# Backward pass of a cached attention block on one core: the last twenty value-cache heads taken two by two

## The chip, the cores and the metric

The kernel runs on one core of a Trainium2 chip. The metric is device time in microseconds for one execution of the whole program, given as the median of several runs. A profiled execution gives, beside its time, a trace of every instruction and DMA packet. The engines of the core are named as in the profile: PE (TensorE, matrix products), PEld (its weight loads), DVE (VectorE), ACT (ScalarE), POOL (GpSimd), SP (SyncE, which only issues loads here). Sixteen DMA engines move data between HBM and the on-chip memory.

## The reference

A pre-norm block with attention over a cache and a small dense layer, for a batch of 2 and one new position, 32 heads of 128, a cache of 4096 positions. The kernel computes the output and all gradients for a given output gradient.

```
def _fwd_reference(A_x, A_k_cache, A_v_cache, A_wq, A_wo, B_x, B_w1, B_w2):
    def _A_ref(x, k_cache, v_cache, wq, wo):
        q = (x @ wq) as [B, 32, 1, 128]
        scores = jnp.einsum("bhqd,bhkd->bhqk", q, k_cache) * (128 ** -0.5)
        p = _softmax(scores, axis=-1)
        o = jnp.einsum("bhqk,bhkd->bhqd", p, v_cache)
        return o as [B, 1, 4096] @ wo
    h = A_x + _A_ref(_layernorm(A_x), A_k_cache, A_v_cache, A_wq, A_wo)
    return h + relu(_layernorm(h) @ B_w1) @ B_w2

_out, _vjp = jax.vjp(_f, A_x, A_k_cache, A_v_cache, A_wq, A_wo, B_w1, B_w2)
_grads = _vjp(grad_out)
```

For one head with scores' softmax p, output gradient go and scaled query q, the large results are two tensors as large as the caches: the V gradient gV[k, d] = p[k] go[d], and the K gradient gK[k, d] = p[k] (V[k] . go - dot) q[d]. All tensors are bf16. K and V are 64 heads of 1 MB each; so are gK and gV.

## The kernel before, in words

**Two passes over the heads.** The first pass reads K and V of every head for the forward result and keeps the unnormalised softmax row of each head in `P_bf`. Once the dense layer's gradient has come back to the attention output, the second pass reads V again, except for twelve heads that are kept on chip, and writes gV and gK. The heads of the second pass stand in the list `turns`; j is a place in it, from 0 to 63. The second pass starts beside the first and is alone from about the middle of the span.

**One head of the second pass** is `p2_iter(j, nsb)` (L869) with its end `p2_tail(j)` (L848), which runs at the start of the next head. A head's V tile `Wt` is 128 partitions by 32 positions by 128 values: a partition's row is 8 KiB and consecutive in HBM (`natural`, L458). PE spreads go and q over all partitions (L878), ACT scales the copy `rb` of both by 1 / sum (L883), and POOL doubles the head's softmax row into `pp` (L885). For dp = V . go, V is transposed in four groups of eight positions (`pair_transpose`, L434: four PE transposes at L442 into one PSUM bank, one ACT copy `t_sb` at L447), and each group is multiplied by go (`pair_matvec`, L450). DVE makes gV by two products of half a tile each (`outer_half`, L841), then in the tail `gsp` = p (dp - dot) (L854) and gK by two more. With `nsb` > 0, ACT makes the last `nsb` of gV's 32 positions instead (L910); before, that is 4 of 32 for each of the last three heads. POOL issues the stores of gV (L911) and gK (L862), 1 MB each; SP issues all loads.

**Buffers.** On-chip tiles of 8 KiB a partition are handed out by tag (`take`, `give`): `ld` for loads, `g` for gV and gK, `f` for output rows of the weight gradients, `q` for the x gradient and the last dense layer. `share` says how many each tag is to own in a stage. When all of the output gradient per head is known (`all_go`), the weights wo are given up and six more tiles come into being (L1194); from then on there are 7 `g` tiles, and 10 when the background work is done.

**Background work.** Generators run a few steps at a time between the steps of a head: `fin_gen` (L984) makes the weight gradients (PE products, ACT copies `ot`, stores on ACT's queue), and `gx_gen` (L1019) the x gradient: it waits for two free `q` tiles, turns the query gradient into two rows `gqr` (PE at L653, ACT at L1043), fetches the five 1 MB pieces of wq (`fetch`, L1025) as `q` tiles come free, and does forty products with sums of 1024 columns on DVE (`ttr`, L669), then a short layer-norm gradient.

**Order.** Nothing is scheduled by a compiler: each engine executes its instructions in the order in which the code records them, so an instruction that waits holds up all behind it on its engine. The main loop (L1183 on) takes one head after another; loads stand in a hand-made `queue` (L1132), and `pump` issues the next as soon as a tile of tag `ld` is free.

Of the kernel before, what the change touches and what calls it, by code (L numbers as in the profile page):

```python
# [7 lines left out]
FP32 = mybir.dt.float32  # L8
# [7 lines left out]
def kernel(  # L16
# [62 lines left out]


    NBIG = 13
    homes = {"ld": list(range(NBIG)), "g": [], "f": [], "q": []}
    free = {tag: len(v) for tag, v in homes.items()}
    owned = dict(free)
    wanted = {}
# [11 lines left out]

    def goes_to(tag):

        if owned[tag] > wanted.get(tag, len(pools)):  # L100
# [333 lines left out]
    def pair_transpose(nat, g, dve=False, busy=0):  # L434
# [12 lines left out]
            nc.scalar.copy(out=t_sb[:], in_=t_ps[:])  # L447
        return t_sb

    def pair_matvec(dst, t_sb, g, vecs):  # L450
        v = t_sb[:].bitcast(BF16).rearrange("p j (k two) -> p j k two", two=2)
        for j in range(GT // 2):
            sc = g * GT + 2 * j
            for par in range(2):
                nc.tensor.matmul(dst[:, sc:sc + 2], lhsT=v[:, j, :, par], rhs=vecs[:, par, :],  # L455
                                 start=(par == 0), stop=(par == 1))
# [4 lines left out]
    def load_tile(what, i, tag):  # L461
        t = take(tag, [128, NSC, 128], what + "t")
        nc.sync.dma_start(out=t[:], in_=natural(A_k_cache if what == "K" else A_v_cache,
                                                *(turns if what == "W" else pairs)[i]))
        (S2 if what == "W" else S1).setdefault(i, {})[what] = t
        (S2 if what == "W" else S1)[i][what + "g"] = tag

    def p1_iter(i, dve_group, busy):

# [378 lines left out]
    def p2_tail(j):  # L848
# [15 lines left out]
        del S2[j]  # L864
        yield

    NSB = 8

    def p2_iter(j, nsb):  # L869

        tail = p2_tail(j - 1) if j - 1 in S2 and "T3" in S2[j - 1] else iter(())
        c = S2[j]
        next(tail, None)
        b, h = turns[j]
# [144 lines left out]
    def gx_gen(fin):  # L1019
# [9 lines left out]
            yield 0.0  # L1029
        while free["q"] < B:  # L1030
            yield 0.0
        banks["o"].remove(6)
        banks["gq"] = [6]
        while 6 in o_busy:
            yield 0.0
        spreading[0] = True
        rows = []
        for b in range(B):
            row = take("q", [128, HD], "gqr")
            for h0 in range(0, H, GH):  # L1040
                t_ps = pst([128, GH * 128], BF16, "gq", "gq_ps")
                spread_cols(t_ps, GQc[:, h0:h0 + GH, b], GH)
                nc.scalar.copy(out=row[:, h0 * 128:(h0 + GH) * 128], in_=t_ps[:])  # L1043
                yield 1.0
            rows.append(row)
        banks["o"].append(6)
        spreading[0] = False
        GW = 1024
# [74 lines left out]
    while i <= NP1 + 1 or j <= NP1:  # L1123
        ii = i if i <= NP1 + 1 else None
        jj = j if i >= NP1 or (i >= P2_AT and (i - P2_AT) % 2 == 0) else None
        plan.append((ii, jj))
        i += 1
        if jj is not None:
            j += 1


    queue = []  # L1132
# [3 lines left out]
    for n, (ii, jj) in enumerate(plan):  # L1136
        if ii is not None:
            if ii < NP1:
                queue.append(("K", ii))
        if ii is not None and ii >= 2:  # L1140
            queue.append(("V", ii - 2))
        ahead = plan[n + 1][1] if n + 1 < len(plan) and ii is not None else jj
        if ahead is not None and ahead < NP1 and turns[ahead] not in kept and ("W", ahead) not in queue:
            queue.append(("W", ahead))
        if ii in W_AT:
            queue.append(("w", W_AT.index(ii)))
        if ii in W2_AT:
            queue.append(("w2", W2_AT.index(ii)))
    def pump():
        while queue:  # L1150
            what, k = queue[0]
            if what == "w":
                load_weights(k)
            else:
                tag = "ld"
                if free["ld"] < 1:
                    return
                if what == "w2":
# [24 lines left out]
    for n, (i, j) in enumerate(plan):  # L1183
# [47 lines left out]
        if i is None:  # L1231
# [76 lines left out]
```

## Time and profile before

| | us |
|---|---|
| median of 3 runs (lowest, highest) | 892.57 (892.43, 893.59) |
| profiled execution | 892.4 |
| its span, first to last instruction | 890.6 |
| busy in the span: PE, weight loads | 740.5, 622.4 |
| busy in the span: DVE, ACT, POOL | 687.8, 469.7, 204.3 |

Moved in the span: 361.84 MB, at 406 GB/s on average; 211.11 MB of it are read from HBM and 149.13 MB written to it. The mean granted clock of TensorE is 0.767 of full speed.

The stores by queue and their time from issue to landing, from the DMA part of the page (tile, queue, count, size, median us):

```
out_dram<-gV POOLq DMA_DIRECT2D x64, 1024.0 KB, 15.1
out_dram<-gK POOLq DMA_DIRECT2D x64, 1024.0 KB, 15.4
Wt<-in_A_v_cache_dram SPq DMA_DIRECT2D x52, 1024.0 KB, 11.8
wqs<-in_A_wq_dram SPq DMA_DIRECT2D x5, 1024.0 KB, 16.1
```

Reading it: a busy share is of the whole span, while the stages differ (first pass, both passes, second pass alone). A DMA share near 1 means that all sixteen DMA engines have packets all the time. "Idle before, and its releaser" is the time that an engine stood still before an instruction and what ended it. Queue q0 is POOL's (the gV and gK stores), q1 SP's (loads), q10 ACT's (weight-gradient stores).

### The profile page before, as it was taken

The page shows a single profiled execution, that of the slowest core. Times are in us where ns is not written, and L with a number is a line of the kernel's source. Part 1 is how long each engine was busy: PE and PEld are TensorE (multiplying, and loading weights), DVE is VectorE, ACT ScalarE, POOL GpSimd, SP SyncE. Part 2 cuts the span into 40 slices and gives each one's busy share as a digit, 9 for nine tenths or more (in the row PEclk, how much of TensorE's full clock was granted, in tenths as well). Part 3 has the DMA queues.
Part 4 walks back from the last instruction along what each step waited for, and adds up shares of the span by engine and source line. Part 5 has one row for each costly group of instructions (what it writes and reads, how often), then busy time and mean ns, then how long its engine had stood idle before and what let it go on. Part 6 is the DMA issues. An engine that isn't in the chain of part 4 may idle for free. (4 is left out here: it accounts for less than half of the span.)

```text
span 890.6 us, 24645 instructions
## 1 busy us (share of the span) xinstructions
PE 740.5 (83%) x10145; PEld 622.4 (70%) x10145; DVE 687.8 (77%) x1283; ACT 469.7 (53%) x1184; POOL 204.3 (23%) x342
## 2 busy tenths in 40 slices
PE   4999899999999998888888767885888888658871
PEld 4887788888887887777777656764666665536561
DVE  2665779876789897796796888786988467899992
ACT  1344334443455665454547766554567766437751
POOL 1344434342310000000023321121323011111141
PEclk9999989999999999997995555555557765555555
DMA  9999999999889999999999999999999999999995
GB/s 377 419 411 404 409 407 419 410 415 408 350 325 369 422 422 424 422 421 424 422 390 423 420 419 420 419 416 416 391 404 413 424 425 425 424 426 424 423 421 245
DMA packets 56304, 361.84 MB, mean 406 GB/s; under 512 B 5696, under 2 KB 11904, under 8 KB 15488
## 3 DMA queue, kind: packets, MB, share of 16 engines
q1 hardware_dynamic: 34536, 211.13, 58.1%
q0 software_dynamic: 18432, 134.23, 36.2%
q10 hardware_dynamic: 3224, 14.92, 4.1%
q8 instruction: 80, 1.31, 0.6%
q14 instruction: 32, 0.26, 0.1%
HBM read 211.11 MB, written 149.13 MB: 404 GB/s over the span
## 5 line engine op out<-in xcount | busy, mean ns | idle before, releaser
L447 ACT COPY t_sb<-t_ps 128x512 f32<-128x512 f32 x479 | 273.1, 587 | 186.3 <-PE t_ps L442 181.7
L455 PEld LDWEIGHTS <-t_sb 128*128 128x128 bf16 x4096 | 169.9, 103 | 83.7 <-ACT t_sb L447 42.3
L442 PE MATMUL t_ps<-ident_f,Wt 128*128 128x128 f32 x832 | 201.0, 393 | 0.4 <-ACT t_sb L447 0.4
L483 DVE TENSOR_TENSOR pk<-Kt,ep 128x2048 bf16<-128x2048 bf16 x128 | 156.2, 1221 | 44.7 <-ACT ep L534 24.9
L476 PE MATMUL m_ps<-pk,Vt 128*128 128x129 bf16 x2048 | 176.1, 223 | 13.3 <-DMA Vt<-in_A_v_cache_dram 12.6
L843 DVE TENSOR_TENSOR gK<-rb,gsp 128x2048 bf16<-128x2048 bf16 x128 | 153.8, 1226 | 28.0 <-DMA out_dram<-gV 26.2
L843 DVE TENSOR_TENSOR gV<-rb,pp 128x2048 bf16<-128x2048 bf16 (+2 forms) x128 | 147.1, 1172 | 30.8 <-DMA out_dram<-gK 24.0
L442 PEld LDWEIGHTS t_ps<-ident_f,Wt 128*128 128x128 f32 x832 | 140.4, 205 | 31.9 <-issue 25.0
L442 PE MATMUL t_ps<-ident_f,Kt 128*128 128x128 f32 x1024 | 154.7, 287 | 4.6 <-DMA Kt<-in_A_k_cache_dram 4.5
L476 PEld LDWEIGHTS <-Vt 128*128 128x128 bf16 x2048 | 131.0, 99 | 16.9 <-DMA Vt<-in_A_v_cache_dram 14.9
L442 PEld LDWEIGHTS t_ps<-ident_f,Kt 128*128 128x128 f32 x1024 | 117.0, 148 | 6.1 <-issue 3.4
L493 POOL COPY pk<-ep 128x16 bf16<-128x16 bf16 x80 | 83.1, 1041 | 151.3 <-ACT ep L534 112.7
L455 PE MATMUL dp_ps<-gom,t_sb 128*128 128x2 bf16 x2048 | 96.0, 168 | 23.3 <-ACT t_sb L447 22.9
L911 POOL DMA_DIRECT2D out_dram<-gV x64 | 34.3, 536 | 307.8 <-DVE nb L526 114.3
L455 PE MATMUL s_ps<-gom,t_sb 128*128 128x2 bf16 x2048 | 80.2, 164 | 1.2 <-DVE t_sb L445 1.2
L862 POOL DMA_DIRECT2D out_dram<-gK x64 | 34.1, 533 | 202.0 <-DVE gK L843 156.8
L593 ACT CAST MT<-m_ps 128x128 bf16<-128x128 f32 x64 | 17.1, 266 | 116.3 <-PE m_ps L476 116.3
L978 ACT CAST ot<-o_ps 128x512 bf16<-128x512 f32 (+3 forms) x152 | 67.0, 498 | 9.7 <-DMA out_dram<-ot 8.5
L883 ACT ACTIVATE rb<-dp_ps,rt 128x256 bf16<-128x256 f32 x64 | 30.2, 472 | 46.5 <-PE dp_ps L878 44.8
L669 DVE CUSTOM_DVE_ANT_0 rows<-wo_t,rows 128x640 bf16<-128x640 bf16 x64 | 52.3, 817 | 0.4 <-ACT rows L647 0.2
L669 DVE CUSTOM_DVE_ANT_0 rows<-wqs,gqr 128x1024 bf16<-128x1024 bf16 x40 | 48.8, 1219 | 0.2
L669 DVE CUSTOM_DVE_ANT_0 rows<-w_t,rows 128x640 bf16<-128x640 bf16 (+2 forms) x58 | 45.8, 790 | 1.2 <-ACT rows L647 0.5
(194 smaller groups left out, 720.4 us busy)
## 6 DMA issues: line engine op xcount, KB each, us to landing
Kt<-in_A_k_cache_dram SPq DMA_DIRECT2D x64, 1024.0 KB, 16.4
Vt<-in_A_v_cache_dram SPq DMA_DIRECT2D x64, 1024.0 KB, 16.6
out_dram<-gV POOLq DMA_DIRECT2D x64, 1024.0 KB, 15.1
out_dram<-gK POOLq DMA_DIRECT2D x64, 1024.0 KB, 15.4
Wt<-in_A_v_cache_dram SPq DMA_DIRECT2D x52, 1024.0 KB, 11.8
out_dram<-ot ACTq DMA_DIRECT2D x6, 960.0 KB, 12.4
wq_t<-in_A_wq_dram SPq DMA_DIRECT2D x5, 1024.0 KB, 11.0
wqs<-in_A_wq_dram SPq DMA_DIRECT2D x5, 1024.0 KB, 16.1
```

Source lines behind the costliest of these rows:

```text
L442: nc.tensor.transpose(t_ps[:, j, :], natf[:, 2 * cc:2 * cc + 2, :].rearrange("p c k -> p (c k)"), ident_f[:])
L447: nc.scalar.copy(out=t_sb[:], in_=t_ps[:])
L455: nc.tensor.matmul(dst[:, sc:sc + 2], lhsT=v[:, j, :, par], rhs=vecs[:, par, :], start=(par == 0), stop=(par == 1))
L476: nc.tensor.matmul(r["m"][:, 0:129], lhsT=r["V"][:, sc, :], rhs=r["pk"][sc // HALF][:, sc % HALF, 0:129], start=(sc == 0), stop=(sc == NSC ...
L483: nc.vector.tensor_tensor(out=p["pk"][k][:, :, 0:128].rearrange("p s (a two) -> p s a two", two=2), in0=p["K"][:, sl, :].rearrange("p s (a ...
L493: nc.gpsimd.tensor_copy(out=col, in_=e)
L669: nc.vector.tensor_tensor_reduce(out=junk[0:kc, 0:width], in0=in0, in1=in1, scale=1.0, scalar=0.0, op0=ALU.mult, op1=ALU.add, accum_out=acc)
L843: nc.vector.tensor_tensor(out=pairs_view(dst[:, sl, :]), in0=row.rearrange("p (a two) -> p a two", two=2)[:, None, :, :].to_broadcast([128 ...
L862: nc.gpsimd.dma_start(out=natural(out_2, bp, hp), in_=gK[:])
L883: nc.scalar.activation(out=rb[:], in_=bank[:, 128:384], func=ACT.Copy, scale=rt[:, b, h:h + 1])
L911: nc.gpsimd.dma_start(out=natural(out_3, b, h), in_=gV[:])
L978: nc.scalar.copy(out=ot[0:P, k, n0:n0 + nn], in_=o_ps[0:P, 0:nn])
```

## The change

From place 44 of `turns` on (`PAIRS_AT`), the twenty last heads, which are neighbours within batch 1, are taken two at a time by new functions `both_iter` and `both_tail`. Both heads lie in one tile of 64 partitions each and 64 positions a partition (`pair_natural`), so that a partition's row is 16 KiB, consecutive in HBM. V comes in two loads of 1 MB, each with 8 KiB of every row (`load_half`). gV and gK of a pair are one tile of 2 MB and one store each; for the last pair each is stored in two halves. There are three tiles of that size, under a new tag `gp`, in the place of the six small ones. The transposes are as before, and each product takes both heads' columns (`both_matvec`), of which each half of the partitions uses its own. Softmax rows now reach `pp` by a PE selection and two ACT copies from PSUM, into slots of `P_bf` that are no longer needed (`spare`); the scale of `rb` is put together by two POOL copies (`by_half`); `gsp` is made in two instructions of 64 partitions.

In `gx_gen` both row tiles are taken at the start, and wq pieces are fetched as tiles come free from then on, while tag `q` gets seven tiles instead of five. ACT makes 8 of the 64 positions of gV for each of the last three pairs. Output-row slots (`slot`) are given by the step of the pair modulo 7.

```diff
+    def both_matvec(dst, t_sb, g, vecs):
+        v = t_sb[:].bitcast(BF16).rearrange("p j (k two) -> p j k two", two=2)
+        for j in range(GT // 2):
+            sc = g * GT + 2 * j
+            for par in range(2):
+                nc.tensor.matmul(dst[:, :, sc:sc + 2], lhsT=v[:, j, :, par], rhs=vecs[:, :, par, :],
+                                 start=(par == 0), stop=(par == 1))
+    def pair_natural(cache, b, h):
+        return cache[b, h:h + 2].rearrange("h (p sc) d -> (h p) sc d", sc=2 * NSC)
+    def load_half(i, k, tag):
+        t = take(tag, [128, NSC, 128], "Wt")
+        nc.sync.dma_start(out=t[:], in_=pair_natural(A_v_cache, *turns[i])[:, k * NSC:(k + 1) * NSC, :])
+        S2.setdefault(i, {})[f"W{k}"] = t
...
+    def spare(k):
+        return P_bf[:, 2 + 4 * k:6 + 4 * k, :].rearrange("p a (s t) -> p (a s) t", t=2)
+    def by_half(dst, src, h):
+        for k in range(2):
+            rows = slice(64 * k, 64 * k + 64)
+            nc.gpsimd.tensor_copy(out=dst[rows], in_=src[rows, h + k:h + k + 1])
+    def both_tail(j):
+        p = S2[j]
+        bp, hp = turns[j]
+        both_matvec(p["dp"], p.pop("T7"), 7, gom[:, bp, hp:hp + 2, :, :])
+        gsp = spare(2)
+        for k in range(2):
+            rows = slice(64 * k, 64 * k + 64)
+            nc.vector.scalar_tensor_tensor(
+                out=gsp[rows], in0=p["dp"][rows, k, :, None].to_broadcast([64, 2 * NSC, 2]),
+                scalar=negdot[rows, hp + k, bp:bp + 1], in1=p["pp"][rows], op0=ALU.add, op1=ALU.mult)
+        yield
+        gK = take("gp", [128, 2 * NSC, 128], "gK")
+        dst = pair_natural(out_2, bp, hp)
+        for k in range(4):
+            outer_half(gK, p["rb"][:, 128:256], gsp, k)
+            if j == NP1 - 2 and k == 1:
+                nc.gpsimd.dma_start(out=dst[:, 0:NSC, :], in_=gK[:, 0:NSC, :])
+            if k < 3:
+                yield
+        if j == NP1 - 2:
+            nc.gpsimd.dma_start(out=dst[:, NSC:2 * NSC, :], in_=gK[:, NSC:2 * NSC, :])
+        else:
+            nc.gpsimd.dma_start(out=dst, in_=gK[:])
+        give(gK)
+        del S2[j]
+        yield
+    def both_iter(j, nsb):
+        tail = tail_of(j)
+        c = S2[j]
+        next(tail, None)
+        b, h = turns[j]
+        go = gom[:, b, h:h + 2, :, :]
+        bank = pst([128, 512], FP32, "sps", "dp_ps")
...
+        rts = Uc[:, 0, j // 2 % 2:j // 2 % 2 + 1]
+        by_half(rts, rt[:, b, :], h)
+        rb = mats.tile([128, 256], BF16, tag="rb", bufs=3, name="rb")
+        nc.scalar.activation(out=rb[:], in_=bank[:, 128:384], func=ACT.Copy, scale=rts)
+        pp = spare(j // 2 % 2)
+        for k in range(2):
+            rows = slice(64 * k, 64 * k + 64)
+            nc.scalar.copy(out=pp[rows].rearrange("p (q s) t -> p q s t", q=2),
+                           in_=pps[rows, k, :, :, None].to_broadcast([64, 2, NSC, 2]))
...
+        for g in range(1, 8):
+            W = c[f"W{g // 4}"]
+            c[f"T{g}"] = pair_transpose(W, g % 4)
+            if g % 4 == 3:
+                give(W)
+            both_matvec(c["dp"], c.pop(f"T{g - 1}"), g - 1, go)
+            if g >= 4:
+                if gV is None:
+                    gV = take("gp", [128, 2 * NSC, 128], "gV")
+                outer_half(gV, c["rb"][:, 0:128], c["pp"], g - 4, HALF - nsb * (g == 7))
+                if nsb:
+                    for k in range((g - 4) * nsb // 4, (g - 3) * nsb // 4):
+                        nc.scalar.activation(out=gV[:, 2 * NSC - nsb + k, :], in_=rb[:, 0:128], func=ACT.Copy,
+                                             scale=pf[:, k:k + 1])
...
+            nc.gpsimd.dma_start(out=pair_natural(out_3, b, h), in_=gV[:])
...
+    PAIRS_AT = 2 * H - 2 * (H - 2 * KEPT[1]) // 2
...
+        rows = [take("q", [128, HD], "gqr") for _ in range(B)]
         banks["o"].remove(6)
...
-        rows = []
-        for b in range(B):
-            row = take("q", [128, HD], "gqr")
+        for b, row in enumerate(rows):
             for h0 in range(0, H, GH):
+                fetch()
...
-            for tag in ("ld", "g", "g", "q", "q", "q"):
-                more_home(tag, big3)
+            for _ in range(3):
+                more_home("gp", big3)
+            assert j == PAIRS_AT
...
-            share(ld=8 + 3 * more, g=7 + 3 * more)
+            share(ld=16)
...
-            share(ld=5 + held + more, g=5 + 2 * more, f=3, q=2 + 3 * more)
+            share(ld=5 + held + int(j > PAIRS_AT), g=5 if not more else 4 * (j == PAIRS_AT), f=3, q=2 + 5 * more)
...
-            nsb = 0 if i is not None else NSB if j < H and fin is None else NSB // 2 if j >= NP1 - 3 else 0
-            g2 = p2_iter(j, nsb) if j < NP1 else p2_tail(NP1 - 1)
+            nsb = 0 if i is not None else NSB if j < H and fin is None else NSB if j >= NP1 - 6 else 0
+            g2 = both_iter(j, nsb) if PAIRS_AT <= j < NP1 else p2_iter(j, nsb) if j < NP1 else both_tail(NP1 - 2)
...
-                slot[0] = int(k in ((1, 3, 5) if j <= H else (1, 4)))
+                slot[0] = int((k if j < PAIRS_AT else k % 7) in ((1, 3, 5) if j <= H else (1, 4)))
```

More of the change, by code (lines that the diff above doesn't have):

```diff
@@ L81 @@
     NBIG = 13
-    homes = {"ld": list(range(NBIG)), "g": [], "f": [], "q": []}
+    homes = {"ld": list(range(NBIG)), "g": [], "f": [], "q": [], "gp": []}
     free = {tag: len(v) for tag, v in homes.items()}
@@ L98, in goes_to @@
     def goes_to(tag):
-        if owned[tag] > wanted.get(tag, len(pools)):
+        if tag != "gp" and owned[tag] > wanted.get(tag, len(pools)):
             for other in homes:
@@ L865, in p2_tail, with tail_of @@
         yield
-    NSB = 8
+    def tail_of(j):
+        if j - 1 in S2 and "T3" in S2[j - 1]:
+            return p2_tail(j - 1)
+        if j - 2 in S2 and "T7" in S2[j - 2]:
+            return both_tail(j - 2)
+        return iter(())
+    def spare(k):
[4 more added lines that the diff above has]
+            nc.gpsimd.tensor_copy(out=dst[rows], in_=src[rows, h + k:h + k + 1])
@@ new lines @@
+    NSB = 8
+    def both_iter(j, nsb):
[5 more added lines that the diff above has]
+        bank = pst([128, 512], FP32, "sps", "dp_ps")
+        for k, col in enumerate((goc, qsc)):
+            for q in range(2):
+                nc.tensor.matmul(bank[64 * q:64 * q + 64, 128 + k * 128:256 + k * 128],
+                                 lhsT=col[:, h + q, b:b + 1].to_broadcast([128, 64]), rhs=ident_bf[:],
+                                 start=True, stop=True)
+        pps = bank[:, 384:512].rearrange("p (k q s) -> p k q s", k=2, q=2)
+        for q in range(2):
+            for k in range(2):
+                nc.tensor.matmul(pps[:, k, q, :], lhsT=sel[:, q, :, :].rearrange("p c k -> p (c k)"),
+                                 rhs=P_bf[:, p_slot[(b, h + k)], :], start=True, stop=True)
+        c["dp"] = bank[:, 0:4 * NSC].rearrange("p (k s) -> p k s", k=2)
+        rts = Uc[:, 0, j // 2 % 2:j // 2 % 2 + 1]
[3 more added lines that the diff above has]
+        pp = spare(j // 2 % 2)
+        for k in range(2):
+            rows = slice(64 * k, 64 * k + 64)
+            nc.scalar.copy(out=pp[rows].rearrange("p (q s) t -> p q s t", q=2),
+                           in_=pps[rows, k, :, :, None].to_broadcast([64, 2, NSC, 2]))
+        if nsb:
+            pf = small.tile([128, NSB], FP32, tag="pf", bufs=2, name="pf")
+            nc.gpsimd.tensor_copy(out=pf[:, 0:nsb], in_=pp[:, 2 * NSC - nsb:2 * NSC, 0])
+        c.update(rb=rb, pp=pp)
+        c["T0"] = pair_transpose(c["W0"], 0)
+        next(tail, None)
+        yield
+        for _ in tail:
+            yield
+        gV = None
+        for g in range(1, 8):
[8 more added lines that the diff above has]
+                outer_half(gV, c["rb"][:, 0:128], c["pp"], g - 4, HALF - nsb * (g == 7))
+                if nsb:
+                    for k in range((g - 4) * nsb // 4, (g - 3) * nsb // 4):
+                        nc.scalar.activation(out=gV[:, 2 * NSC - nsb + k, :], in_=rb[:, 0:128], func=ACT.Copy,
+                                             scale=pf[:, k:k + 1])
+                if j == NP1 - 2 and g == 5:
+                    nc.gpsimd.dma_start(out=pair_natural(out_3, b, h)[:, 0:NSC, :], in_=gV[:, 0:NSC, :])
+            yield
+        if j == NP1 - 2:
+            nc.gpsimd.dma_start(out=pair_natural(out_3, b, h)[:, NSC:2 * NSC, :], in_=gV[:, NSC:2 * NSC, :])
+        else:
+            nc.gpsimd.dma_start(out=pair_natural(out_3, b, h), in_=gV[:])
+        give(gV)
+        yield
+        yield
@@ L869, in p2_iter @@
+    PAIRS_AT = 2 * H - 2 * (H - 2 * KEPT[1]) // 2
     def p2_iter(j, nsb):
-        tail = p2_tail(j - 1) if j - 1 in S2 and "T3" in S2[j - 1] else iter(())
+        tail = tail_of(j)
         c = S2[j]
@@ L1044, in gx_gen @@
                 yield 1.0
-            rows.append(row)
         banks["o"].append(6)
@@ L1128 @@
         if jj is not None:
-            j += 1
+            j += 2 if PAIRS_AT <= jj < NP1 else 1
     queue = []
@@ L1143 @@
         if ahead is not None and ahead < NP1 and turns[ahead] not in kept and ("W", ahead) not in queue:
-            queue.append(("W", ahead))
+            queue += [("X", (ahead, 0)), ("X", (ahead, 1))] if ahead >= PAIRS_AT else [("W", ahead)]
         if ii in W_AT:
@@ L1157, in pump @@
                     return
-                if what == "w2":
+                if what == "X":
+                    load_half(*k, tag)
+                elif what == "w2":
                     w2_tiles[k] = load_w2(k, tag)
@@ L1208 @@
                 bg_until(("go", *turns[j]))
-            nsb = 0 if i is not None else NSB if j < H and fin is None else NSB // 2 if j >= NP1 - 3 else 0
-            g2 = p2_iter(j, nsb) if j < NP1 else p2_tail(NP1 - 1)
+                assert j < PAIRS_AT or ("go", *turns[j + 1]) in done
+            nsb = 0 if i is not None else NSB if j < H and fin is None else NSB if j >= NP1 - 6 else 0
+            g2 = both_iter(j, nsb) if PAIRS_AT <= j < NP1 else p2_iter(j, nsb) if j < NP1 else both_tail(NP1 - 2)
         elif open_tail:
```

## The prediction

> **What bounds the kernel now.** I read the forty slices first. DMA is nine tenths or more almost everywhere, so the question is only where it is not, and what the bytes cost.
>
> ```profile
> DMA  9999999999889999999999999999999999999995
> GB/s 377 419 411 404 409 407 419 410 415 408 350 325 369 422 422 424 422 421 424 422 390 423 420 419 420 419 416 416 391 404 413 424 425 425 424 426 424 423 421 245
> ...
> q1 hardware_dynamic: 34536, 211.13, 58.1%
> q0 software_dynamic: 18432, 134.23, 36.2%
> ```
>
> The reader sees a flat 420 to 426 GB/s from slice 31 on, and a last slice at half. The queues' shares (58.1 + 36.2 + 4.1 + 0.6 + 0.1) add to 99.1%: sixteen DMA engines are busy for 882.6 of 890.6 us. Then the busy times by stretch, from 700 us, which is where the first changed head (turn 44, its gV store issued at 705.7) stands. Columns: stretch, length, busy us of PE, its weight loads, DVE, ACT, POOL, then granted clock, DMA share, GB/s.
>
> ```profile
> 700.00:750.00 50.00, 42.60 (x444) 32.07 (x444) 30.24 (x35) 34.42 (x73) 7.47 (x16) 0.64 1.01 426
> 750.00:800.00 50.00, 30.96 (x262) 22.41 (x260) 44.39 (x66) 22.15 (x51) 7.42 (x15) 0.53 1.01 425
> 800.00:850.00 50.00, 43.06 (x360) 29.54 (x359) 46.87 (x63) 36.15 (x73) 7.34 (x15) 0.57 1.01 424
> 850.00:875.00 25.00, 17.46 (x174) 15.02 (x174) 24.24 (x40) 12.23 (x28) 11.38 (x17) 0.50 1.01 419
> 875.00:880.00 5.00, 0.00 (x0) 0.00 (x0) 0.00 (x0) 0.00 (x0) 0.44 (x1) 0.50 1.01 419
> 880.00:882.00 2.00, 0.00 (x0) 0.00 (x0) 0.00 (x0) 0.00 (x0) 0.00 (x0) 0.50 0.53 221
> 882.00:885.00 3.00, 0.00 (x0) 0.00 (x0) 0.00 (x0) 0.00 (x0) 0.00 (x0) 0.50 0.07 30
> 885.00:888.00 3.00, 0.00 (x0) 0.00 (x0) 0.00 (x0) 0.00 (x0) 0.00 (x0) 0.50 0.06 27
> ```
>
> Three things. DMA is never idle to 880 (1.01, since neighbouring packets overlap by some ns). From 750 to 875 DVE is busy 115.5 of 125 us: it is nearly a second bound. And from 882 to 888 the share is 0.06, one sixteenth: **one of the sixteen DMA engines ends about six microseconds after the others**, and the span is its span. The trace's completion marks say the same: the sixteenth mark of the last store comes at 888.9, the fifteenth 5.97 us earlier.
>
> Last, what DVE does from 700 us, and its waits (busy us, mean ns, idle before):
>
> ```profile
> L669 DVE CUSTOM_DVE_ANT_0 rows<-wqs,gqr 128x1024 bf16<-128x1024 bf16 x40 | 48.8, 1219 | 0.2
> L843 DVE TENSOR_TENSOR gK<-rb,gsp 128x2048 bf16<-128x2048 bf16 x40 | 47.9, 1226 | 12.9 <-DMA out_dram<-gV 12.5
> L843 DVE TENSOR_TENSOR gV<-rb,pp 128x2048 bf16<-128x2048 bf16 x37 | 44.3, 1219 | 13.5 <-DMA out_dram<-gK 9.7 <-ACT ot L978 3.5 <-ACT GQr L938 0.3
> L854 DVE SCALAR_TENSOR_TENSOR gsp<-dp_ps,negdot,P_bf 128x64 bf16<-128x64 f32 x20 | 5.6, 278 | 1.7 <-PE dp_ps L455 1.7
> L843 DVE TENSOR_TENSOR gV<-rb,pp 128x1536 bf16<-128x1536 bf16 x3 | 2.8, 944 | 0.0
> ```
>
> DVE's idle time is waits for store buffers (12.5 + 9.7 us), nearly all before 795. The engines that compute wait for DMA, not DMA for them. So an edit counts by what it takes off the DMA engines, the latest one above all, as long as DVE keeps them fed.
>
> **The change part by part, against the profiled execution's 892.4 us** (span 890.6 and 1.8 around it; the median of the runs is 0.17 higher).
>
> *Packets.* The 40 last gV and gK stores of 1 MB become 18 of 2 MB with 16 KiB rows and, for the last two heads, 4 of 1 MB in halves, which keep 8 KiB pieces. The bytes are the same. Each DMA engine has 8 rows of a tile, so 18 x 16 = 288 packets of 8 KiB become 144 of 16 KiB. No store packet of 16 KiB is in the trace. The rows near it: packets of 8 KiB take 309 ns and of 4 KiB 159 ns (the packet records, medians; the 4 KiB ones are the wq gradient's). So 4 KiB more cost 150 ns and 9 ns are per packet, or 6 ns by the distance from start to start (306). Saved: 144 x 6 to 9 ns = 0.9 to 1.3 us, and 18 completion marks less at 6 to 9 ns, 0.1 to 0.2. Bounds 1.0 and 1.5; I take 1.1, nearer the distances, which are what adds up. The V loads are still 1 MB in 8 KiB rows.
>
> *The late engine.* From 853 to 872 its completion marks are 2.59 to 2.64 us apart for each 1 MB store; after 874, when nothing more is issued, 2.44 to 2.46. So while stores are being issued it loses about 0.16 us for each. By the marks its distance to the next engine grew from 2.9 us at 703 to 6.0 at 872. If the loss goes with the number of stores or their pieces, 18 fewer save up to 18 x 0.16 = 2.9 us; if it goes with bytes, nothing. The growth over these 40 stores was 3.1 us, and with half the pieces it would be about half: 1.3 to 1.5. I take 1.3, near the middle, since no row parts the two.
>
> The Trainium skill, DMA: Bandwidth & Descriptors, section Latency and other measured facts, says that two of sixteen engines are usually slower, with contention for the descriptor rings that GpSimd's queue keeps in SBUF as its best guess. By that, the loss goes with descriptors and the high end (2.9) would hold, 888.4 us; the trace shows one clearly late engine, not two, and does not name it, so I lean on it no further.
>
> *DVE.* The same 160 products of half a tile's width at 1.22 us. gsp becomes 20 instructions on 64 partitions and 128 elements; not shown. Bounds 0.28 (as now) and 0.56 (twice); from 0.17 us for 10 elements (the small tensor operations) to 0.28 for 64, about 0.41: +2.6 us in all. The last three gV tiles lose 1024 of their elements instead of three heads losing 512: 3 x 0.6 against 3 x 0.28, -1.0. Sum +1.6 us on DVE, 0 on the path while DMA is the bound.
>
> *ACT and POOL.* ACT: 24 columns of gV instead of 12 (at 0.39, in the rows 3.8 us for 12: +4 to 5), ten rb fewer (-4.7), 20 small copies for pp from PSUM (0.25 to 0.59 each, as the nearest copies: +5 to 12). It is busy 105 of 175 us there: 0. POOL drops 20 pp copies (0.47) and adds 20 of one column. PE: as many transposes and products with the pair's two heads in one product (4 columns for 2), and four selections for each pair at about 0.3 us: 12 us over 170, behind DMA: 0.
>
> *A new wait.* rb of a pair now needs a scale that two POOL copies make, and these stand in POOL's queue behind the issue of the previous pair's gV store, which waits for DVE. Behind rb on ACT wait the pp copies, the pair's first t_sb and any output copies; behind those PE's products, and behind them gsp. Cost hidden, as DVE then has gK, the next gV and up to eight x-gradient products to do (10 to 20 us).
>
> *x gradient.* Its rows and four of five wq pieces come before later V loads on SP's queue. Three pairs of V halves are already ahead of the first piece, and another one before the next three. 4 MB in front are 10 us at 424 GB/s, 20 at half of it, against three pairs of some 17 us each (170 us for ten) of loads ahead: 0. The 40 products (48.8 us) end at head 57 instead of 59, so DVE has them in its idle time of 700 to 750 (19.8 us) rather than at the end, which pays for the 1.6 us.
>
> *Buffers.* Store buffers go from seven to ten of 1 MB to three of 2 MB. When DVE may refill one, two are still queued: 4.2 MB at 424 GB/s is 9.9 us, 15 or more beside loads. DVE makes a tile in 5.2 us, about 10.4 with four x-gradient products. So 0, by a thin margin.
>
> Sum: 892.4 - 1.1 - 1.3 = **890.0 us**.
>
> **Rivals.**
> - *Packets only (or not even cut fewer):* the late engine's loss goes with bytes: 892.4 - 1.1 = 891.3; if the rows are split again at 8 KiB, 892.3. For: its cause is not visible. Against: its marks close up when issuing ends.
> - *The engines end together:* DVE can now run at most three tiles ahead of the slowest engine, and another mix of queues spreads its burden: up to the whole 5.97 us goes, 892.4 - 1.1 - 6.0 = 885.3. For: early in the kernel the sixteen marks stand within 5 us. Against: work is dealt evenly, and waiting does not remove an engine's own loss.
> - *Slower: the new wait serialises the pairs.* From gV's end: issue 0.53, POOL copies 0.9, rb 0.47, pp 0.6, then eight groups at 1.25 us (the last heads' pace on PE), a copy 0.59: 13 us to gsp; then gK and the next gV, 10 us. Two pairs in 23, 11.5 each, where DVE alone needs 10; with outputs mixed in a group takes 2 us and it is up to 3 more for each. At 1.5 to 3 us over ten pairs DVE ends 15 to 30 us after today's 874.6. It decides only once DVE ends after about 883, since the late engine hides the first 8 us: with 15 us, 890 + 5 for the last landing + 1.8 = 897. For: DVE is 92% busy from 750 and three buffers hold less in hand. Against: while x-gradient products lie between, DVE's own pair takes 20 us.
> - *Slower: 16 KiB packets are slow.* The only ones in the trace, 80 of instruction queue q8, are 0.6% of 16 engines' span: 1.07 us each, against 0.62 for two of 8 KiB. 144 x 0.45 = 65 us, 957. Against: their destination is another memory.
>
> **How the numbers follow.** Forecast 0.44 (its own range from both terms' better bounds, 888.0, to 890.8, where what is left is hardly more than the packets); engines together 0.12; packets only or none 0.20; serialised pairs 0.20; slow packets 0.04. 0.2% is 1.8 us, about what a measurement of this kernel can tell from no change; so faster (below 890.8) 0.56, same 0.20, slower 0.24. The range takes in the forecast, packets only, most of the engines-together case and the nearer half of the serialised pairs: 886 to 896. The likeliest case's own range is 888 to 891.
>
> **What would show it.** Stores of 16 KiB packets near 609 ns; DMA share 1.01 to about 879; completion of the late engine within 4 to 5 us of the next. The x-gradient products over by head 57, DVE's last product by 877. Wrong: a DMA share under 1.0 between 700 and 870, long waits of rb for POOL or of gsp for PE, 16 KiB packets over 620 ns.

## The result, and the profile after

| | us |
|---|---|
| changed kernel, median of 6 runs (lowest, highest) | 901.83 (901.08, 903.85) |
| kernel before, median of 6 runs beside it | 893.39 (892.43, 894.35) |
| ratio, 95% interval | 1.0099 (1.0084 to 1.0113) |
| profiled execution, its span | 901.2, 899.4 |

The change makes the kernel 8.4 us slower; forecast were 2.4 us less, with a range of 886 to 896. First the changed kernel's slices and queues:

```profile
DMA  9999999999989999999999999999999999999986
GB/s 377 419 410 404 410 406 419 410 413 407 351 339 374 421 423 424 422 424 423 414 402 419 413 419 419 416 416 419 388 422 412 424 420 422 423 380 353 406 348 281
...
q1 hardware_dynamic: 34536, 211.13, 57.9%
q0 software_dynamic: 15840, 134.22, 35.9%
```

Queue q0 has 2592 packets fewer for the same bytes, as counted: 2304 of 16 KiB in the place of 4608, and the completion packets of 18 stores. But slices 36, 37 and 39 are at 380, 353 and 348 GB/s, where before had 421 to 426. The busy times by stretch (columns as before: stretch, length, PE, its loads, DVE, ACT, POOL, clock, DMA share, GB/s):

```profile
700.00:750.00 50.00, 41.23 (x420) 32.09 (x418) 39.99 (x50) 32.01 (x68) 6.60 (x12) 0.64 1.01 421
750.00:800.00 50.00, 28.23 (x289) 20.76 (x290) 39.10 (x56) 22.87 (x58) 4.14 (x8) 0.57 1.01 420
800.00:850.00 50.00, 38.07 (x294) 24.08 (x293) 41.88 (x60) 30.24 (x64) 6.67 (x10) 0.57 0.95 372
850.00:875.00 25.00, 18.71 (x185) 14.16 (x184) 18.12 (x29) 16.16 (x42) 7.25 (x9) 0.64 0.84 346
875.00:880.00 5.00, 4.61 (x53) 4.42 (x54) 5.00 (x5) 2.90 (x7) 2.13 (x3) 0.52 0.96 400
880.00:885.00 5.00, 2.29 (x41) 1.64 (x38) 1.64 (x4) 3.47 (x10) 0.53 (x1) 0.82 0.93 383
885.00:890.00 5.00, 0.00 (x0) 0.00 (x0) 3.71 (x4) 0.00 (x0) 1.07 (x2) 0.50 0.96 395
```

DVE is busy 99.1 of the 125 us from 750 to 875, where it had 115.5; from 700 to 750 it is ahead (39.99 for 30.24). From 800 on the DMA engines run dry: the share is short of its earlier 1.01 by 0.06 of 50 us, 0.17 of 25 and some 0.06 of 15, which makes 8 us idle. What DVE waits for from 690 us on (waiting line and releaser: us in all, times, longest; "P_bf L907" is `gsp`, which now stands in spare slots of `P_bf`):

```profile
DVE P_bf L907 <- PE dp_ps L455: 23.1, 6, 7.7
DVE gK L859 <- DMA out_dram<-gK: 8.8, 1, 8.8
DVE ml L752 <- PE mlp_ps L748: 7.2, 3, 4.4
```

Before, 28.2 of DVE's 34.1 us of waits were for store buffers: DVE waited because DMA was behind, which is free. Now 12.0 of 46.8 us are, and the rest, 34.8 us, can keep stores from DMA. How much of it does so, this view does not tell. DVE's last product ends at 888.7 instead of 874.6.

Two waits that before does not have are seen on ACT (start, duration, line, and in brackets the idle time before and its releaser):

```profile
770.35 0.34 ACTq L1106 DMA_DIRECT2D out_dram<-ot  x1
770.73 0.59 ACT L447 COPY t_sb<-t_ps 128x512 f32<-128x512 f32 x1 [9.32 <-DMA Wt<-in_A_v_cache_dram]
...
784.25 0.34 ACTq L1106 DMA_DIRECT2D out_dram<-ot  x1
784.63 0.22 ACT L1050 COPY wide<-x1c 128x32 bf16<-128x32 bf16 x1 [7.67 <-DMA wqs<-in_A_wq_dram]
```

ACT stands twice, 17 us in all, before it issues a weight-gradient store, until a *load of SP* has landed. In the trace the DMAs of SP and ACT take eight completion counters in turn (100 to 104 and 107 to 109), and each issue waits for the DMA that had its counter last. The V halves issued at 725 and 727, behind four wq pieces, landed after 38 and 44 us, and the wq piece issued at 742 after 43.

Another loss lies behind the last store. Waits of SP at the end of the program, changed kernel, then before:

```profile
SPq L1431 <- PEq L1431: 4.6, 2, 4.1
```

```profile
SPq L1303 <- PEq L1303: 1.0, 2, 0.5
```

The view puts it down to PE's sequencer; the trace's single events name POOL. The last completion mark comes at 894.1, SP reaches the closing barrier of all engines at 894.72, and POOL, which releases it, does so at 898.70: 3.98 us later. Before it was 0.36. POOL's entry just before the release is a `DRAIN`, which ends at 898.65. So of the 8.8 us by which the span grew, 3.6 are this pause and 5.2 a later last landing. In those 5.2: 8 us of idle DMA and some 5 of packets that took longer than the median of their size (6.3 us an engine from 700 on, before 0.9), less 1.1 for larger packets, 5.4 as the late engine's lag fell from 5.97 to 0.55, and 1.7 by which this execution was ahead before the change begins (the same store issue of POOL stands at 651.5 and 653.3).

### The profile page after: what moved, and what is told of

Its sections match the earlier page's. It is cut to its first block, busy times and chain, and to the rows that moved or that the text cites. A ratio compares the mean times of both kernels' runs of the same rounds, so it can differ in the third digit from the quotient of the medians.

```text
span 899.4 us, 24699 instructions
## 1 busy us (share of the span) xinstructions
PE 737.2 (82%) x10185; PEld 616.9 (69%) x10185; DVE 688.9 (77%) x1283; ACT 472.3 (53%) x1206; POOL 197.5 (22%) x324
## 5 line engine op out<-in xcount | busy, mean ns | idle before, releaser
L442 PE MATMUL t_ps<-ident_f,Wt 128*128 128x128 f32 x832 | 197.9, 387 | 0.4 <-ACT t_sb L447 0.4
L442 PEld LDWEIGHTS t_ps<-ident_f,Wt 128*128 128x128 f32 x832 | 136.3, 200 | 29.2 <-issue 24.7
L442 PE MATMUL t_ps<-ident_f,Kt 128*128 128x128 f32 x1024 | 152.8, 285 | 4.1 <-DMA Kt<-in_A_k_cache_dram 3.8
L492 PEld LDWEIGHTS <-Vt 128*128 128x128 bf16 x2048 | 130.6, 99 | 17.4 <-DMA Vt<-in_A_v_cache_dram 15.5
L859 DVE TENSOR_TENSOR gK<-rb,gsp 128x2048 bf16<-128x2048 bf16 x88 | 105.7, 1226 | 22.1 <-DMA out_dram<-gV 11.8
L859 DVE TENSOR_TENSOR gV<-rb,pp 128x2048 bf16<-128x2048 bf16 x88 | 100.2, 1160 | 19.3 <-DMA out_dram<-gK 10.9
L463 PE MATMUL dp_ps<-gom,t_sb 128*128 128x2 bf16 x1408 | 65.3, 167 | 20.6 <-ACT t_sb L447 20.3
L1036 POOL DMA_DIRECT2D out_dram<-gV x44 | 23.6, 537 | 232.2 <-DVE nb L542 113.7
L878 POOL DMA_DIRECT2D out_dram<-gK x44 | 23.5, 533 | 142.4 <-DVE gK L859 112.2
L859 DVE TENSOR_TENSOR gK<-rb,P_bf 128x2048 bf16<-128x2048 bf16 x40 | 47.4, 1221 | 1.5 <-DMA out_dram<-gV 1.2
```

Source lines behind the costliest of these rows:

```text
L442: nc.tensor.transpose(t_ps[:, j, :], natf[:, 2 * cc:2 * cc + 2, :].rearrange("p c k -> p (c k)"), ident_f[:])
L492: nc.tensor.matmul(r["m"][:, 0:129], lhsT=r["V"][:, sc, :], rhs=r["pk"][sc // HALF][:, sc % HALF, 0:129], start=(sc == 0), stop=(sc == NSC ...
L859: nc.vector.tensor_tensor(out=pairs_view(dst[:, sl, :]), in0=row.rearrange("p (a two) -> p a two", two=2)[:, None, :, :].to_broadcast([128 ...
L878: nc.gpsimd.dma_start(out=natural(out_2, bp, hp), in_=gK[:])
L1036: nc.gpsimd.dma_start(out=natural(out_3, b, h), in_=gV[:])
```

## The experiments

Three edits were made to the changed kernel, one by one and in combination. O undoes a part of the change: the x gradient's order as before. S and P are repairs: S makes the scale of `rb` a pair earlier, so that it does not stand behind POOL's store; P has POOL issue the weight-gradient stores of the pair stage instead of ACT, which issues them in the kernel before too. "Pause" is POOL's release of the closing barrier after SP's arrival, "gsp" DVE's wait for PE there from 690 on; both from the profiled execution. That one can lie off its run's median, by 4.9 us at most (e14: 910.33). Ratios are to the kernel before, run beside each.

| run | edit | median us | ratio (95%) | pause | gsp |
|---|---|---|---|---|---|
| | changed kernel | 901.83 | 1.0099 (1.0084, 1.0113) | 3.98 | 23.1 |
| e1 | O | 897.59 | 1.0058 (1.0023, 1.0093) | 3.98 | 12.2 |
| e2 | S | 901.81 | 1.0112 (1.0087, 1.0137) | 3.98 | 15.7 |
| e3 | O, S | 897.42 | 1.0054 (1.0039, 1.0069) | 3.98 | 6.8 |
| e4 | P | 895.80 | 1.0034 (1.0020, 1.0048) | 0.49 | 17.4 |
| e9 | P, O | 892.91 | 0.9996 (0.9983, 1.0008) | 0.49 | 13.2 |
| e10 | P, S | 894.70 | 1.0022 (1.0009, 1.0035) | 0.49 | 16.1 |
| e5 | P, O, S | 893.07 | 0.9992 (0.9980, 1.0005) | 0.49 | 5.0 |
| e6 | P, O, S, stores in halves | 894.68 | 1.0010 (0.9997, 1.0022) | 1.33 | 13.9 |
| e7 | P, O, S, ACT's eighth undone | 894.13 | 0.9997 (0.9984, 1.0009) | 0.49 | 6.7 |
| e12 | P, O, S, later loads | 893.22 | 0.9994 (0.9981, 1.0007) | 0.49 | 7.3 |
| e13 | two stores on POOL | 902.86 | 1.0107 (1.0083, 1.0131) | 4.40 | 15.6 |
| e14 | the other nine on POOL | 905.39 | 1.0156 (1.0131, 1.0182) | 0.07 | 17.3 |
| e17 | stores in halves | 901.85 | 1.0096 (1.0078, 1.0115) | 0.36 | 25.1 |
| e15 | P, O, two small DMAs a load | 895.00 | 1.0028 (1.0012, 1.0043) | 0.49 | 7.1 |
| e16 | P, O, one small DMA a load | 893.60 | 1.0001 (0.9987, 1.0015) | 0.49 | 8.0 |
| e8 | before, early x gradient | 892.23 | 0.9987 (0.9976, 0.9999) | 0.36 | 12.3 |
| e11 | before, five store buffers | 893.52 | 1.0004 (0.9992, 1.0017) | 0.36 | 5.6 |
| e18 | before, both of these | 893.00 | 1.0007 (0.9995, 1.0018) | 0.36 | 1.7 |

**The order, the scale, and both (e1, e2, e3).**

```diff
-        rows = [take("q", [128, HD], "gqr") for _ in range(B)]
         banks["o"].remove(6)
...
-                fetch()
...
-            share(..., q=2 + 5 * more)
+            share(..., q=2 + 3 * more)
```

```diff
-        by_half(rts, rt[:, b, :], h)
+        if j == PAIRS_AT:
+            by_half(rts, rt[:, b, :], h)
+        if j + 2 < NP1:
+            b2, h2 = turns[j + 2]
+            by_half(Uc[:, 0, (j // 2 + 1) % 2:(j // 2 + 1) % 2 + 1], rt[:, b2, :], h2)
```

> The changed kernel with its x-gradient part put back (rows taken one after the other, no wq piece fetched while the rows are made, five q tiles instead of seven). Theory L (late loads): in the changed kernel four wq pieces stand before the V loads, a V load of 725 us lands 38 to 40 us later, and ACT's output stores, which wait for the DMA that used the same completion counter before, hold ACT for 9.3 and 7.7 us; with the order put back these two waits go, gsp's waits for PE (23 us) fall under 10, and the time falls by 5 to 9 us, to 893 to 897. Theory W (the new wait of rb for POOL serialises the pairs): no gain, 900 to 903. Theory B (three store buffers of 2 MB hold too little): no gain, 900 to 903.

> The changed kernel with the two POOL copies of a pair's scale made one pair earlier, so that rb no longer waits behind the previous pair's gV store. Theory W: rb's waits for POOL (15 us) go, gsp's waits for PE fall under 8 us, time 894 to 897. Theory L: rb's waits go but the V loads are as late as before and ACT stands as long; 899 to 902. Theory B: 900 to 903.

> The changed kernel with both of these: x-gradient order put back and scale made a pair ahead. L and W together: 889 to 893, and the DMA share is 1.0 up to the end of the stores. L alone: as the kernel with the order put back, within 1 us. W alone: as the kernel with the scale ahead, within 1 us. B: at least 898.

The order is worth 4 us. The scale is worth nothing: e2 takes rb's waits for POOL from 15.0 to 6.3 us and gsp's from 23.1 to 15.7, yet DVE then waits for the dense layer's late pieces of w2 (12.0 us at `ml` instead of 7.2). In the other three pairs of runs that differ by S alone, rb's waits for POOL fall further (28.4 to 1.7 from e1 to e3, 17.5 to none from e4 to e10, 21.6 to 4.3 from e9 to e5), for 0.4 to 1.1 us, which is within the noise. So the serialised pairs, as the prediction told them, are not the cause. Both signs that it had named for being wrong are there, though: a DMA share under 1.0 before 870 and long waits of gsp for PE.

**The stores on POOL (e4), and with the others (e5, e9, e10).**

```diff
-            nc.scalar.dma_start(out=out_v[:, c0:c0 + gn, :], in_=ot[0:P, 0:gn, :])
+            (nc.gpsimd if late[0] else nc.scalar).dma_start(out=out_v[:, c0:c0 + gn, :], in_=ot[0:P, 0:gn, :])
```

> The changed kernel with the weight-gradient stores of the pair stage issued by POOL instead of ACT, so that ACT no longer waits for the completion counters of SP's loads; the V loads stay as late. Theory L in its strict form (ACT's wait is what costs): ACT's waits for V and wq loads (17 us) go, and 3 to 7 us are gained, 895 to 899. If the late loads cost through PE's own wait for V: no gain, 900 to 903, with PE waiting for V loads instead. Theories W and B: 900 to 903; POOL's queue, which now also waits for ACT's copies, may cost 1 to 2 us.

> The changed kernel with three edits: the weight-gradient stores of the pair stage issued by POOL, the x gradient's rows and wq pieces in the order of before, and the scale made a pair earlier. If ACT's wait on SP's loads (6 us) and the order of loads (about 3 us beyond it) add up, the time is 892 to 893.5, level with before, and no instruction of ACT waits for a load. If both were the same wait seen twice (with the old order no ACT instruction waited for a load either), the time stays at 895 to 896.5 and what is left is the pairs' own: gK waiting 7 us or more for a store buffer, gsp waiting for PE, DVE ending after 883.

> The changed kernel with the weight-gradient stores on POOL and the old order of the x gradient, but the scale made as the change has it. If ACT's wait and the order add up and the new wait of rb costs nothing, the time is that of all three edits, 892 to 894. If the scale's wait only shows once the other two are out of the way, it is 894.5 to 897 and rb waits for POOL 15 us or more between 700 and 890.

> The changed kernel with the weight-gradient stores on POOL and the scale a pair earlier, the x gradient fetched first as in the change. If fetching first still costs 2 to 3 us when ACT no longer waits for loads (late V halves, slow packets from 810 to 840), the time is 895 to 897 against 893 with all three edits. If fetching first costs only through ACT's wait, it is 892.5 to 894.

P alone gives 6 us, P and O together bring the kernel level with before, and S adds nothing in any company. Busy times of e9 (P and O):

```profile
800.00:850.00 50.00, 42.23 (x339) 28.43 (x337) 44.55 (x61) 34.33 (x74) 9.31 (x14) 0.57 0.99 412
850.00:875.00 25.00, 18.68 (x199) 16.30 (x199) 21.79 (x37) 14.71 (x37) 7.05 (x12) 0.57 0.95 393
```

DVE is busy 66.3 of these 75 us where the changed kernel has 60.0, and the DMA share is 0.99 and 0.95 for 0.95 and 0.84. Averaged over the four pairs of runs that differ by one edit, as differences of the ratios times 893: O is worth 3.7 us (2.7 to 5.2), P 6.2 (5.5 to 8.0), S 0.2 (-1.2 to 1.1). In brackets are the lowest and the highest of the four; by the intervals of the eight ratios each average is good to about 1.2 us either way. Of P's 6.2, 3.5 are the pause (3.98 to 0.49 in each of the four); 2.7 remain for the stores themselves.

**What the pause goes with.** Over all twenty traces it goes with the number of DMAs that POOL issues in the whole program: it is 3.98 us in the four with 110 (the changed kernel, e1, e2, e3), 4.40 with 112 (e13), 0.07 with 119 (e14), 0.49 in the eight with 121, 0.36 in the five with 128 (before among them) and 1.33 with 139 (e6). The change takes 18 DMAs from POOL, 128 to 110, by storing pairs at once; e17 puts those 18 back by halving the stores, and the pause is 0.36 again. Why these numbers of DMAs give these pauses, the traces do not show.

**Which stores (e13, e14).** Only the two whose issue stood (`nth` counts the eleven), and, with `not in`, only the others:

```diff
+            nth[0] += late[0]
-            nc.scalar.dma_start(...)
+            (nc.gpsimd if late[0] and nth[0] in (4, 5) else nc.scalar).dma_start(...)
```

> The changed kernel with only two of its eleven weight-gradient stores of the pair stage issued by POOL: the fourth and fifth, whose issue on ACT stood at 761 to 770 and 777 to 784 us. Theory waits (ACT's issue stands for a load eight DMAs earlier, as completion counters go round): nearly all of the gain of moving all eleven is here, 895.5 to 897.5, and ACT shows no wait for a load. Rival queues (what counts is that the stores leave their own DMA queue and no longer take a share beside the V loads): two of eleven give a sixth to a fifth of the 6 us, 900.5 to 901.

> The complement: the other nine are issued by POOL, the fourth and fifth stay on ACT. Theory waits: ACT still stands for loads there (their counters are now those of somewhat other loads), and the time is 899 to 903. Rival queues: 896 to 897.5.

Both theories fall. With the two moved, no ACT instruction waits for a load any more, and the time does not fall; the largest waits of DVE in e13 show where it went:

```profile
DVE ml L753 <- PE mlp_ps L749: 15.7, 3, 8.1
DVE P_bf L908 <- PE dp_ps L456: 15.6, 7, 5.3
```

`ml` is what DVE makes of the w2 products, and PE itself stood for the w2 pieces (`w_t`). PE's longest wait in e13, then the same wait in the changed kernel:

```profile
PE mlp_ps L749 <- DMA w_t<-in_B_w_dram: 17.3, 3, 8.5
```

```profile
PE mlp_ps L748 <- DMA w_t<-in_B_w_dram: 4.0, 1, 4.0
```

PE executes in order, so V's transposes stand behind those products. The wait is 11 to 20 us in e2, e4, e10, e13 and e14, which all keep the early x gradient. With the old order it is absent before and in e1, 2.4 us in e9 and 5.8 in e5, but 11.3 in e3. It is 1.3 us in e17, which is no faster for it.

With nine moved it even rises, though the pause is gone. Moving some of the stores also shifts which DMAs share a counter: SP stood 29 and 35 us for its own earlier loads in these two (28 in the changed kernel, 0 in e5 and e9).

**Is it SP's standing (e15, e16)?** P and O, with two DMAs of 256 bytes before each V half (in e16 one) that use up counters:

```diff
         t = take(tag, [128, NSC, 128], "Wt")
+        for x in range(2):
+            nc.sync.dma_start(out=out_3[turns[i][0], turns[i][1] + k, x:x + 1, :], in_=ident_bf[x:x + 1, :])
```

> The kernel with the weight-gradient stores on POOL and the old order (893, and SP never stood for a load of its own), with two more DMAs of 256 bytes on SP's queue before each of the pairs' V halves; they write bytes that the pair's store writes again. Theory counters on SP: eight counters go round over SP's and ACT's DMAs, an issue waits until the DMA eight places before it has landed, so with three DMAs to a V half SP may have fewer than three loads under way; SP stands for its own DMAs 15 us or more between 680 and 850, V comes late, the time rises by 4 to 12 us to 897 to 905. Rival: the number of DMAs under way does not matter, 40 DMAs of 256 bytes cost nothing to speak of: within 1 us of 893.

> The same with one such DMA before each V half: four halves under way at most. Theory counters on SP: between nothing and half of what two do, 893 to 898, in step with the time for which SP stands for its own DMAs. Rival: within 1 us of 893.

SP now stands for its own DMAs; the largest waits in e15, from 680 to 850:

```profile
SPq L482 <- DMA Wt<-in_A_v_cache_dram: 29.4, 8, 4.6
...
SPq L482 <- DMA wqs<-in_A_wq_dram: 20.1, 4, 7.0
```

In all 76 us in e15 and 48 in e16, and the price is 2.9 and 0.4 us (ratios less that of e9). By proportion, SP's 28 us in the changed kernel are worth 0.2 us (by e16) to 1 us (by e15).

**Stores in halves, ACT's eighth, later loads (e17, e6, e7, e12).**

```diff
-        if j == NP1 - 2:
+        if True:
             nc.gpsimd.dma_start(out=dst[:, NSC:2 * NSC, :], in_=gK[:, NSC:2 * NSC, :])
```

```diff
-            nsb = ... NSB if j >= NP1 - 6 else 0
+            nsb = ... NSB // 2 if j >= NP1 - 3 else 0
```

```diff
-            share(ld=16)
+            share(ld=4, x=12)
```

> The changed kernel with every pair's gV and gK stored in two halves of 1 MB, so that store packets are 8 KiB again beside V packets of 8 KiB. Theory counters on SP with the share of the packets: the V loads landed late (38 to 40 us) because store packets were twice theirs; with equal packets loads land sooner, SP's waits for its own loads fall from 28 us to under 12, ACT's from 17 to under 6, and the time falls to 895 to 899. Rival, the size of the packets does not matter for the loads: 901.5 to 903 (dearer packets by 1 us), SP's and ACT's waits as in the changed kernel.

> The kernel with the three edits, and every pair's gV and gK stored in two halves of 1 MB (8 KiB pieces), as the change does for its last pair alone. Theory buffers: a 2 MB tile is stored only when all four products are done, so a buffer is away for the products and a landing of 10 us after them; halves start the store two products (2.4 us) earlier, so gK's wait for a buffer shrinks by 2 to 5 us and the time falls by 1 to 3 us against the three edits alone, the 1 us of dearer packets (144 more at 6 to 9 ns) included. Rival, packets: buffers do not decide, the time rises by about 1 us. The store packets of 8 KiB are near 309 ns in both cases.

> The kernel with the three edits, and ACT makes 4 of the 64 positions of gV in the last pair alone instead of 8 in each of the last three pairs (ACT does 20 columns fewer, 8 us at 0.39 us each; DVE does 1.3 us more). If ACT's part delays gV's store (POOL waited 10.8 us for it once in the changed kernel) the time falls by 1 to 3 us. If DVE sets the end, it rises by up to 1.3 us. If neither, within 0.5 us.

> The kernel with all three edits, with four load tiles in place of sixteen after the x gradient, so that the last V halves are fetched later and lie beside the stores. If the end is short of DMA work because the loads are over at 845 and stores alone come no faster than DVE and PE make them (5.2 us for 2 MB against 4.9 on the DMA engines), the share after 850 rises to 1.0 and the time falls by 1 to 2 us to 891 to 892. If what DVE makes sets the end, it stays within 0.7 us of 893; if V halves then come late for PE, it rises by 1 to 4 us and PE waits for loads of V.

In e17 loads do land sooner (SP's waits for them fall from 28 to 6 us, ACT's from 17 to 5) and the pause is gone, and still the time stays, so the halves lose elsewhere what the pause gave. What remains is gsp, at 25.1 us the longest of all, and the share in the stretch from 840 to 860 was 0.77. In the repaired kernel the halves cost 1.6 us (e6 less e5), of which 0.8 is a longer pause, the rest about the price of 144 packets. ACT's eighth and the moment of the last loads decide nothing.

**Before, with parts of the change (e8, e11, e18).** e8 is the first diff above the other way round, put into the kernel before, with five `q` tiles as it had; e11 is this one, and e18 both:

```diff
-            share(ld=8 + 3 * more, g=7 + 3 * more)
+            share(ld=8 + 3 * more, g=7 - 2 * more, x=5 * more)
...
-            share(..., g=5 + 2 * more, ...)
+            share(..., g=5, x=2 * more, ...)
```

> The kernel before with only the x-gradient edit: both row tiles taken at the start and wq pieces fetched as tiles come free. Tag q still gets five tiles, so three pieces go ahead instead of three after the rows. If early pieces are a loss by themselves (they delay V loads, and ACT's stores share counters with SP's loads), the time rises by 1 to 4 us and ACT shows waits for loads. If the loss needs the pairs' thin supply (three buffers, no store backlog), it is within 1 us of before, with the DMA share 1.01 to 880.

> The kernel before with five store buffers of 1 MB for the second pass's last stage in place of seven to ten; nothing else. If the late DMA engine ends level with the others only because a thin supply makes the others wait for it, its lag at the end falls from 6 us to 3 or less here too, while the time does not fall: the DMA share drops below 1.0 after 800, DVE waits more for buffers and ends later than 874.6, and the time is 893 to 899. If depth of supply decides nothing, the lag stays near 6 and the time within 1 us of before.

> The kernel before with the x-gradient edit and with five store buffers of 1 MB in the last stage; heads one by one. If it is the thin supply of store buffers that makes the early x gradient costly (its products no longer fill DVE's waits near the end, and no backlog of stores covers them), the time rises by 2 us or more over the two edits apart (892.2 and 893.5), and DVE waits for PE at gsp 10 us or more. If the cost needs the pairs' own chain (V halves, eight groups to one gsp, scale on POOL), it stays within 1.5 us of before.

With heads one by one, neither the early x gradient nor fewer store buffers costs anything, nor both. In e8 gsp waits 12.3 us for PE, and it costs nothing either. e8 is the one version whose interval lies wholly below before, by 0.01 to 0.24%. In e11, DVE's waits:

```profile
DVE gK L843 <- DMA out_dram<-gK: 16.6, 8, 5.6
DVE gV L843 <- DMA out_dram<-gV: 12.8, 9, 4.0
DVE gsp L854 <- PE dp_ps L455: 5.6, 3, 2.9
```

In this execution (895.43 us, 1.9 above e11's median) DVE ends 7.6 us later than before, at 882.2, and the late engine's lag is 3.3 us instead of 6.0: the fifteenth mark of the last store comes 5.7 us later than before, the sixteenth 3.0 later. The lag closes because the others end later.

## Why the prediction was wrong

**Packets, right.** 16 KiB packets took 611 ns against 309 for 8 KiB, 7 ns saved for each pair; forecast were 609. The rival of slow packets is out. DVE's own work was right too: its new gsp takes 7.0 us in all, where 8.2 were counted. Of a gain, the repaired versions e5, e7, e9 and e12 show 0.3 to 0.7 us, none beyond its interval.

**The late engine: the term of 1.3 us does not exist.** I took its lag at the end for time that could be had. The lag does shrink, to 0.55 us in the changed kernel and 1.75 to 3.5 in e5, e7, e9 and e12, but in e11 it shrinks to 3.3 without any larger store and without a gain. A lag measures how far the others are ahead, not what the last one has to do. Nor was it a steady loss before: it stood at 8.5 us at 835, 5.0 at 859 and 6.0 at the end. The Trainium skill (DMA: Bandwidth & Descriptors, Latency and other measured facts) gives contention for descriptor rings as its best guess for slower engines. I drew from it that fewer pieces lighten them; no run here shows that. The rival "engines end together" was right about the marks and gave 885.3; its price fell with the same step.

**"x gradient ... 0": the failed step that cost 3.7 us.** I compared bytes in front with the loads that SP already had ahead, and found 10 to 20 us against three pairs. The V halves behind the pieces landed 38 to 44 us after issue. The w2 pieces, which stand in the same queue and which I did not count at all, landed at 754 and 787 instead of 727 and 766 to 769, and where ACT does not stand, PE stands for them (17.3 us in e13, 19.9 in e10). Late V halves alone are not the price: in e9, level with before, those issued from 724 to 780 take 28 to 38 us too. Nor is the wait for w2 all of it, by e17. And the 40 products, which I was glad to see move forward, ended at 842.8 for 850.1 before: DVE did 10 us more from 700 to 750, when it had time, and 16 us less from 750 to 875. "Pays for the 1.6 us" counted work and not when it is there to fill a wait. With heads one by one nearly the same edit (five `q` tiles, not seven) costs nothing (e8, e18), so it is not early loads as such.

**"Buffers ... 0, by a thin margin".** The margin went, but not by the buffers: DVE's waits for them fell from 28 to 12 us. Five small buffers instead of seven to ten are free (e11), and with the early x gradient too (e18). Three large ones may take away what covers other waits, for between 853 and 872 before there were always stores under way; no run parts that from the rest of the pairs.

**A new wait: the right place and nearly the right time, for the wrong reason.** The rival had DVE end at 889.6 and the kernel at 897; DVE ended at 888.7, at gsp waiting for PE. But its cause, rb behind POOL's store, is worth 0.2 us (S). What the pairs do bring is a chain of eight groups to one gsp instead of four; that each delay of PE, ACT or a V half is met by DVE at once in it is my reading, which no run isolates. Its links replace each other: with rb early (e2) or ACT's two waits gone (e13) DVE waits for w2, with 8 KiB packets (e17) for gsp again. No single wait that was taken away gained anything; the order undone and all stores off ACT together end it.

**Not in the sum at all: ACT's stores and the program's end.** I counted queues that the loads were moved past on SP, and not that ACT's issues wait for SP's loads through shared counters. All eleven on POOL are worth 2.7 us beside the pause; through which wait is open, since taking ACT's two waits away gained nothing in e13 (where PE stood for w2 instead) and e15 leaves about 1 us to SP's. No run has P in the kernel before, so it is not shown either that the change loses these 2.7 us rather than that the edit would gain them anywhere. The pause of 3.6 us could be had from no row of before. It belongs to the packets' step, which gave fewer stores nothing but a gain of 0.1 to 0.2 us for their marks: the 18 DMAs fewer on POOL go with 3.6 us more at the end.

**The sum, mended.** 892.4 - 1.1 (packets, not resolved from the medians) + 3.6 (pause) + 3.7 (order) + 2.7 (stores on ACT) = 901.3, against 901.2 for the profiled execution and a median of 901.83. Order and stores are good to about 1.2 us each. That the parts were averaged over partners and still add up is some support, no proof.

## What to carry to other kernels

A DMA share of 1.01 says that compute has slack, not how much: sort the slack engine's waits into those for DMA, which are free, and the others, and ask which of the others the change lengthens. Here the first kind went from 28 to 12 us, the second from 6 to 35. The second kind says where to look and is no price: e9, level with before, has 32 us of it. When undoing one part gains nothing, undo it in combination before dropping it, and look behind the last landing: 3.6 of this loss's 8.4 us lay there.

## What the runs showed of the hardware that was not expected

- POOL released the closing barrier 3.98 us after SP's arrival in four programs, 4.40 in one, 1.33 in one and 0.07 to 0.49 in fourteen. Programs with the same number of DMAs issued by POOL had the same pause to 0.01 us (110: 3.98; 121: 0.49; 128: 0.36).
- Beside store packets of 16 KiB, loads in packets of 8 KiB got less: from 720 to 740 q1 moved 1.5 MB in 10 us and q0 2.4 MB, while before both moved 1.95; in e17, with stores in packets of 8 KiB again, q1 moved 1.95 and q0 1.97.
- While loads moved 1.0 to 1.5 MB in 10 us, from 790 to 840, their packets took 2.6 us an engine longer in all than their median of 309 ns, against 0.02 before; in e17 it was 1.1. The cause is not shown.
